# One slice's two layer-1 weight pieces converted by instructions over 1024 columns, and a query transposition that takes its result buffers itself

## The chip, the cores and the metric

The kernel runs on one core of a Trainium2 chip. A core has a matrix engine (TensorE, in the profile PE for matmuls and PEld for loading their weights), a vector engine (DVE), a scalar engine (ACT), GpSimd (POOL) and an engine that here only starts DMAs (SP). Each runs its own instructions in their order and waits on semaphores for the others. The metric is the device time of one execution in microseconds (us), lower is better. What is compared is the median of several runs; a profile is of one execution.

## The reference

```python
def _attn_ref(q, k, v, f):                      # 4 batches, 8 heads, 576 tokens, 64 per head
    scores = scale * np.matmul(q, k.transpose(0, 1, 3, 2))
    log_f = np.log(np.clip(f, 0.0001, 1.0))
    cum = np.cumsum(log_f, axis=-1)
    decay = cum[:, :, :, None] - cum[:, :, None, :]
    scores = np.where(causal, -1000000000.0, scores + decay)
    attn = softmax(scores)
    return np.matmul(attn, v)

def _moe_ref(x, w_in, w_out, alpha):            # layer 1: 2304 x 512, 512 x 2048, 2048 x 512
    h = x @ w_in
    g = np.maximum(h, 0.0) + alpha * np.minimum(h, 0.0)
    return g @ w_out

def _moe2_ref(x, w_in, w_out):                  # layer 2, same sizes
    h = x @ w_in
    g = np.where(h >= 1, h, np.where(h <= -1, 0.0, (h + 1) ** 2 / 4))
    return g @ w_out

def reference(...): return moe2(moe(attention(q, k, v, f)))
```

The weights arrive as 64-bit floats. The kernel has to make 32-bit values of them itself, from the two 32-bit words of each number.

## The kernel before

Attention runs batch by batch in units of 256 and 320 queries, and in each unit over four pairs of heads. The scores of a head (`ps_s`) are copied out by ACT with the decay as bias (L670), masked by POOL (L460), reduced to a maximum by DVE (L689, L707) and POOL (L713), subtracted (DVE, L729), exponentiated (ACT, L732) and multiplied with v (`ps_o`). The sums are inverted by way of a small DMA round trip (`rec`, `spread`, `sums`), and the result becomes a part of `x` (L837, L846, L849). The first batch uses plain 32-bit matmuls; from the second on operands are split in a high and a low part, as all of the weights and layer activations are.

Layer 1 goes through 9 chunks of 256 tokens and in each through 16 slices of 128 hidden units. For a slice, PE makes `ps_h` from the slice's part of w_in (12 matmuls, L979), ACT and DVE make `g` and its two parts (L989, L992, L998, L1001), and PE adds to `ps_y` with the slice's part of w_out (12 matmuls, L1018). Layer 2 takes the chunks in one narrow step of 256 tokens and four wide ones of 512 (`ps_h` L1154, `g` L1167 to L1182, `ps_z` L1201).

The weights of a layer come in 32 pieces of 128 x 512: piece 2s is the part of w_in for slice s, piece 2s + 1 that of w_out. A piece is loaded by SP (`raw`, L883), and then turned into 32-bit values: ACT writes the absolute value of the upper word to `val` (L894), DVE clamps it (L897), shifts it (L906), puts sign and top bits in (L914) and the lowest bits (L919), ACT copies the high part to `w` (L927) and DVE subtracts to get the low part (L932). Layer 1's pieces are done while attention begins, in buffers named `w0` to `w31` that hold raw words, `val` and at last `w` of different pieces one after the other; the raw words of piece i lie in the buffer of piece i + 2. Layer 2's pieces go to the same `w` buffers when the last chunk of layer 1 has used what is in them (`w_use`), by way of 3 raw and 14 `val` buffers.

The order of instructions on each engine is not that of the program text. Every step is a task with an engine, an assumed duration, a position (`pos`), dependencies and the ring buffers that it takes or uses. A planner (`Order.emit`) goes through assumed time, and gives each engine, whenever it is free, the task with the lowest position of those that can start. A task that takes a buffer is only given when one is free. Attention of the first batch has negative positions, conversions of layer 1 the position of their slice in the first chunk minus 9 or so, so that they fill what attention leaves. The waits in the program follow from the data and the buffers, not from the planner's assumed times.

Query transposition, from the second batch on: PE transposes the queries of a head into one of three PSUM buffers shared with the scores (`qtr`, L577), ACT copies the high part out (`qhi`) and DVE the low part (`qlo`); there are two result buffers per head of a pair, and it is `qhi` that takes them.

Of the kernel before, what the change touches and what calls it, by code (L numbers as in the profile page):

```python
# [16 lines left out]
P = 128  # L17
# [174 lines left out]
def kernel(  # L192
# [36 lines left out]
    AHEAD = 2  # L229
    THROTTLE = 8  # L230
    X2T = 768
# [232 lines left out]
    for u, pr in head_list():  # L464
# [104 lines left out]
        for j in range(0 if plain else 2):  # L569
# [18 lines left out]

            a = add("PE", 112 * np_, qtr, pos_of(2 * pr + j) - 1, [T["lq"], last.get("qtr")], new=[pb], use=[qb_])
            last["qtr"] = a  # L590
            h = add("ACT", act(n), qhi, pos_of(2 * pr + j) - 1, [a], new=qb, use=[pb])
            qready[j] = [h, add("DVE", dve(n), qlo, pos_of(2 * pr + j) - 1, [h], use=[pb, *qb])]
# [272 lines left out]
    W = {}  # L865
    W_ready = {}

    def convert(layer, i, pos, raw_ring, slot, deps, wdeps):
# [4 lines left out]
        there = layer == 1 and i + AHEAD < NPIECE  # L873
        vb = Buf(Ring(1) if there else R["val1" if layer == 1 else "val2"])
        keep = rb if there or not wide else vb

        def load():
            if part == 0:
                src = win[:, s * P:(s + 1) * P].rearrange("(c p) f -> p c f", p=P)
            else:  # L880
                src = wout[s * P:(s + 1) * P, :].rearrange("p (c f) -> p c f", f=P)
            rb.t = slot(rb)
            nc.sync.dma_start(out=rb.t, in_=src)  # L883
            if layer == 1 and i == 2:
                nc.sync.dma_start(out=alpha_sb, in_=alpha.rearrange("(s p) -> p s", p=P))

# [4 lines left out]
        def mag():  # L891
            pool, tag = (wpool, f"w{i}") if there else (ph["p"] if layer == 1 else P2["p"], f"val{vb.slot}")
            vb.t = pool.tile([P, DM], F32, tag=tag, name="val")
            nc.scalar.activation(out=vb.t, in_=words()[1].bitcast(F32), func=AF.Abs)  # L894
# [6 lines left out]
        def low_exp():  # L901
            if layer == 1 and i == 6:
                nc.vector.tensor_scalar(
                    out=calpha, in0=alpha_sb, scalar1=-1.0, scalar2=1.0, op0=ALU.mult, op1=ALU.add)
            bits = vb.t.bitcast(I32)
# [4 lines left out]
        def word():  # L910
            return words()[1] if there else vb.t.bitcast(I32)

# [12 lines left out]
        def hi():  # L925
            w = wpool.tile([P, 2, DM], F32R, tag=f"w{i}", name="w")
            nc.scalar.copy(out=w[:, 0, :], in_=val())  # L927
            W[layer, i] = (w[:, 0, :], w[:, 1, :])
# [7 lines left out]
        if wide:  # L936
            a = add("ACT", act(DM), mag, pos, [a] + (wdeps if layer == 1 else []), new=[vb], use=[rb])
            a = add("DVE", dve2(DM), clamp, pos, [a], use=[vb])
# [10 lines left out]
    raw_users = {}  # L949
    for i in range(NPIECE):  # L950
        def slot(b, i=i):
            return wpool.tile([P, NCC, P], WT, tag=f"w{i + AHEAD if i + AHEAD < NPIECE else i}", name="raw")

        r = convert(1, i, l1_pos[0, i // 2] + i % 2 / 2 - 1 + WOFF, Ring(1), slot,
                    raw_users.get(i - (THROTTLE if i + AHEAD < NPIECE else AHEAD), []),
                    raw_users.get(i - AHEAD, []))
        raw_users[i] = r
        conv1 += r
    for t in order.tasks:
        if "convert" in t.deps:  # L960
# [107 lines left out]
    for i in range(NPIECE):  # L1068
        conv2 += convert(2, i, NF * NC1 + i / 2 + WOFF2, R["raw2"],
                lambda b: P2["p"].tile([P, NCC, P], WT, tag=f"raw{b.slot}", name="raw"), [t_open], w_use[i])  # L1070

# [200 lines left out]
```

## Time and profile before

| | |
|---|---|
| runs (us) | 1062.47, 1063.72, 1067.35; median 1063.72 |
| profiled execution | 1062.05 us, its span 1060.3 us, mean granted clock of PE 0.985 |
| busy, share of the span | PE 96%, PEld 87%, DVE 71%, ACT 62%, POOL 14% |
| HBM | 61.42 MB read, 9.51 MB written |

The span goes from the first to the last instruction of the core; some 1.75 us of the execution lie outside of it. A busy share is an average over stages that have different limits: the first 160 us hold the first batch's attention and all of layer 1's conversion, up to some 560 us attention and layer 1 run side by side, and from 700 us on there is only layer 2.

### The profile page before, as it was taken

Reading aid. Unit: us, or ns where it says so; the run is one execution under the profiler, and the core shown is the slowest. Engines: PE = TensorE matmul, PEld = TensorE weight load, DVE = VectorE, ACT = ScalarE, POOL = GpSimd, SP = SyncE. Lnnn points to the kernel's source line nnn. Section 1 sums busy time; section 2 is a strip of 40 time slices with the busy share of each in tenths; the row PEclk is TensorE's granted clock in tenths of the full one; section 3 lists DMA queues with packets and bytes.
Section 4 is the critical chain, followed back from the end, with each engine's and each line's share of the span. In section 5 each row is a group of like instructions: output and inputs, shape, how many; then the busy total and the mean of one; then the engine's idle time right before and its main releaser. Section 6 shows DMA issues by size and latency. Waiting matters only on the chain.

```text
span 1060.3 us, 19265 instructions
## 1 busy us (share of the span) xinstructions
PE 1017.5 (96%) x6531; PEld 922.1 (87%) x6531; DVE 753.3 (71%) x1901; ACT 653.5 (62%) x1734; POOL 143.2 (14%) x239
## 2 busy tenths in 40 slices
PE   5679989999999999999999999999999999999998
PEld 3448879999999999999999999988888888888886
DVE  7989997787777787787757989974454445444443
ACT  6868778888888888987854465653343333333233
POOL 3323223211322113321200000000000000000000
PEclk9869999999999999999999999999999999999999
DMA  8774122311132111331105633521011001000001
GB/s 242 183 233 121 43 73 66 69 44 48 32 80 61 45 48 33 75 72 38 39 7 166 189 111 121 160 79 41 1 40 41 0 1 40 1 1 31 11 1 40
DMA packets 125650, 72.27 MB, mean 68 GB/s; under 512 B 89424, under 2 KB 119120, under 8 KB 125552
## 3 DMA queue, kind: packets, MB, share of 16 engines
q1 hardware_dynamic: 125552, 71.04, 24.6%
q8 instruction: 52, 0.85, 0.3%
q14 instruction: 46, 0.38, 0.1%
HBM read 61.42 MB, written 9.51 MB: 67 GB/s over the span
## 4 chain that ended last, share of the span: by engine, by line
PE 81%; DVE 5%; ACT 5%; issue 4%; DMA 3%; SPq 1%; POOL 1%; POOLq 0%; ACTq 0%; DVEq 0%
PE ps_h L1154 19%; PE ps_z L1201 18%; PE ps_y L1018 16%; PE ps_h L979 16%; PE ps_s L656 3%; PE ps_o L766 2%; PE ps_o L772 1%; PE ps_o L774 1%; PE ps_o L773 1%; PE pst L577 1%; DMA sums<-spread 1%; DMA spread<-rec 1%; SPq L404 1%; PE ps_s L652 1%; DMA raw<-in_k_dram 1%
## 5 line engine op out<-in xcount | busy, mean ns | idle before, releaser
L979 PE MATMUL ps_h<-x,w 128*128 128x256 f32 x1728 | 235.8, 286 | 4.3 <-DVE g L992 2.2
L1018 PE MATMUL ps_y<-gH,w 128*128 128x256 f32 x1152 | 236.3, 288 | 0.0
L979 PEld LDWEIGHTS ps_h<-x,w 128*128 128x128 f32 x1728 | 218.5, 192 | 6.5 <-DVE g L992 3.8
L1018 PEld LDWEIGHTS ps_y<-gH,w 128*128 128x128 f32 x1152 | 189.9, 192 | 0.2
L1154 PE MATMUL ps_h<-xw,w 128*128 128x512 f32 x768 | 184.5, 389 | 0.0
L1201 PE MATMUL ps_z<-w,gH 128*128 128x512 f32 x576 | 177.7, 389 | 0.0
L1154 PEld LDWEIGHTS ps_h<-xw,w 128*128 128x128 f32 x768 | 144.2, 188 | 29.9
L1018 PE MATMUL ps_y<-gL,w 128*128 128x256 f32 x576 | 163.7, 284 | 2.4 <-DVE gL L1001 2.4
L1179 ACT CAST gH<-g 128x256 fp32r<-128x256 f32 x144 | 58.5, 407 | 160.7 <-PE ps_z L1201 160.0
L1182 DVE TENSOR_TENSOR gL<-g,gH 128x256 fp32r<-128x256 f32 x144 | 61.0, 424 | 124.7 <-ACT gH L1179 124.5
L1201 PEld LDWEIGHTS ps_z<-w,gH 128*128 128x128 f32 x576 | 107.1, 188 | 21.4
L1171 ACT ACTIVATE g<-g,half 128x256 f32<-128x256 f32 x144 | 73.3, 509 | 69.9 <-DVE g L1167 69.6
L1018 PEld LDWEIGHTS ps_y<-gL,w 128*128 128x128 f32 x576 | 110.5, 192 | 3.3 <-DVE gL L1001 3.0
L1201 PE MATMUL ps_z<-w,gL 128*128 128x512 f32 x288 | 112.0, 389 | 0.0
L460 POOL TENSOR_SCALAR_AFFINE_SELECT S<-S 128x128 f32<-128x128 f32 (+1 forms) x160 | 61.3, 387 | 336.3 <-ACT S L670 319.7
L670 ACT ACTIVATE S<-ps_s,nb 128x320 f32<-128x320 f32 (+3 forms) x224 | 99.6, 449 | 11.3 <-PE ps_s L656 7.8
L992 DVE SCALAR_TENSOR_TENSOR g<-g,calpha,ps_h 128x256 f32<-128x256 f32 x144 | 68.3, 477 | 32.2 <-ACT g L989 31.4
L1174 DVE TENSOR_TENSOR g<-ps_h,g 128x256 f32<-128x256 f32 x144 | 61.0, 424 | 40.5 <-ACT g L1171 39.8
L713 POOL PARTITION_ALL_REDUCE Mb<-Mx x64 | 80.5, 1258 | 59.6 <-DVE Mx L707 24.2
L732 ACT ACTIVATE S<-S 128x320 f32<-128x320 f32 (+1 forms) x192 | 79.5, 423 | 11.7 <-DVE S L729 10.9
L729 DVE TENSOR_TENSOR S<-Mb,S 128x320 f32<-128x320 f32 (+3 forms) x224 | 78.7, 397 | 9.7 <-POOL Mb L713 9.1
L998 ACT CAST gH<-g 128x256 fp32r<-128x256 f32 x144 | 58.1, 405 | 42.4 <-DVE g L992 33.8
(100 smaller groups left out, 1607.8 us busy)
## 6 DMA issues: line engine op xcount, KB each, us to landing
raw<-in_moe_w_in_dram SPq DMA_DIRECT2D x32, 512.0 KB
raw<-in_moe_w_out_dram SPq DMA_DIRECT2D x32, 512.0 KB
x<-ysb SPq DMA_DIRECT2D x36, 128.0 KB
x<-x SPq DMA_DIRECT2D x9, 512.0 KB
out_dram<-osb SPq DMA_DIRECT2D x18, 256.0 KB
qr<-in_q_dram SPq DMA_DIRECT2D x64, 64.0 KB
raw<-in_k_dram SPq DMA_DIRECT2D x32, 128.0 KB
raw<-in_v_dram SPq DMA_DIRECT2D x24, 128.0 KB
```

Of the source, the lines that this page charges most:

```text
L460: nc.gpsimd.affine_select(out=sl, in_=sl, pattern=[[1, sl.shape[1]]], compare_op=ALU.is_ge, fill=NEG, base=base, channel_multiplier=-1)
L670: nc.scalar.activation(out=Sb.t[:, so:so + m], in_=sb.t[:, :m], func=AF.Identity, bias=bias)
L713: nc.gpsimd.partition_all_reduce(Mb.t[:, :n], Mx.t[:, :n], P, ReduceOp.max)
L729: nc.vector.tensor_tensor(out=sl, in0=Mb.t[:, qo:qo + m], in1=sl, op=ALU.subtract)
L732: ex = add("ACT", act(gn), lambda Sb=Sb, gn=gn: nc.scalar.activation(out=Sb.t[:, :gn], in_=Sb.t[:, :gn], func=AF.Exp, scale=-SCALE), pb_, ...
L979: nc.tensor.matmul(out=hb.t, lhsT=a[:, sl], rhs=b, start=(cc == 0 and t == 0), stop=(cc == NCC - 1 and t == 2))
L992: nc.vector.scalar_tensor_tensor(out=gb.t, in0=gb.t, scalar=calpha[:, s:s + 1], in1=hb.t, op0=ALU.mult, op1=ALU.add)
L1018: nc.tensor.matmul(out=Y[c][e // 2][:, e % 2, :], lhsT=a[:, sl], rhs=b, start=(s == 0 and t == 0 and e % 2 == 0), stop=(s == NF - 1 and t ...
L1154: nc.tensor.matmul(out=hb.t, lhsT=a[:, sl], rhs=b, start=(cc == 0 and t == 0), stop=(cc == NCC - 1 and t == 2))
L1171: nc.scalar.activation(out=gb.t, in_=gb.t, func=AF.Square, scale=0.5, bias=half)
L1174: nc.vector.tensor_tensor(out=gb.t, in0=hb.t[:, hs], in1=gb.t, op=ALU.max)
L1201: nc.tensor.matmul(out=zb[tg].t, lhsT=a[:, sl], rhs=b, start=(s == 0 and t == 0), stop=(s == NF - 1 and t == 2))
```

## The change

Slices 0 to 11 of layer 1 get one raw buffer for both pieces (still two DMAs), one `val` and one `w`, and each of the seven conversion steps is one instruction over 1024 columns. Slices 12 and 13 have their raw words in the four single buffers `p28` to `p31`, so that only the clamp and the shift are one instruction over 1024; their other five steps are two of 512 each. Slices 14 and 15 are converted piece by piece as before. Both pieces of a slice are ready together (`W_ready`), and the second load depends on the first in the planner. Layer 2's two pieces of slices 0 to 13 share one `w` buffer too, so each piece now waits for the last use of both. `qtr` now takes the two result buffers that `qhi` took. `THROTTLE` counts slices in place of pieces.

```diff
-    THROTTLE = 8
+    THROTTLE = 4
...
-            a = add("PE", 112 * np_, qtr, pos_of(2 * pr + j) - 1, [T["lq"], last.get("qtr")], new=[pb], use=[qb_])
+            a = add("PE", 112 * np_, qtr, pos_of(2 * pr + j) - 1, [T["lq"], last.get("qtr")], new=[pb] + qb, use=[qb_])
             last["qtr"] = a
-            h = add("ACT", act(n), qhi, pos_of(2 * pr + j) - 1, [a], new=qb, use=[pb])
+            h = add("ACT", act(n), qhi, pos_of(2 * pr + j) - 1, [a], use=[pb, *qb])
...
+    NWIDE = NF - 2 * AHEAD if wide else 0
+
+    def convert1(s, pos, deps, wdeps):
+        one = s < NWIDE
...
+                        rb.t = wpool.tile([P, 2, NCC, P], WT, tag=f"w{s + AHEAD}", name="raw")
...
+                nc.sync.dma_start(out=raws[-1][:, part if one else 0], in_=src)
...
+            loads.append(add("SP", 500, load, pos - 2 + part / 2, deps + loads, new=[] if part else [rb],
+                             use=[rb] if part else [], move=moved(P, 4096) if part else moved(NCC * P, 1024)))
...
+        n = 1 if one else 2
+        m = 2 * DM // n
+        a = add("ACT", n * act(m), lambda: each(mag), pos, loads + wdeps, new=[vb], use=[rb])
+        a = add("DVE", dve2(2 * DM), clamp, pos, [a], use=[vb])
+        a = add("DVE", dve2(2 * DM), low_exp, pos, [a], use=[vb])
+        a = add("DVE", n * dve(m), lambda: each(top), pos, [a], use=[vb, rb])
+        a = add("DVE", n * dve(m), lambda: each(bottom), pos, [a], use=[rb])
+        h = add("ACT", n * act(m), lambda: each(hi), pos, [a] + wdeps, use=[rb])
+        l = add("DVE", n * dve(m), lambda: each(lo), pos, [h], use=[rb])
+        W_ready[1, 2 * s] = W_ready[1, 2 * s + 1] = [h, l]
...
-            w = wpool.tile([P, 2, DM], F32R, tag=f"w{i}", name="w")
+            if s < NF - AHEAD:
+                if s not in WS2:
+                    WS2[s] = wpool.tile([P, 2, 2, DM], F32R, tag=f"w{s}", name="w")
+                w = WS2[s][:, part]
+            else:
+                w = wpool.tile([P, 2, DM], F32R, tag=f"p{i}", name="w")
...
+    for s in range(NF - AHEAD):
+        r = convert1(s, l1_pos[0, s] - 0.75 + WOFF, raw_users.get(s - THROTTLE, []), raw_users.get(s - AHEAD, []))
...
         conv2 += convert(2, i, NF * NC1 + i / 2 + WOFF2, R["raw2"],
-                lambda b: P2["p"].tile([P, NCC, P], WT, tag=f"raw{b.slot}", name="raw"), [t_open], w_use[i])
+                lambda b: P2["p"].tile([P, NCC, P], WT, tag=f"raw{b.slot}", name="raw"), [t_open],
+                w_use[i - i % 2] + w_use[i - i % 2 + 1])
```

Because the planner orders every engine anew, instructions move everywhere. The clamp is L914 in the new file, the shift L923, the next two L928 and L933, the low part L948 (L987, L993, L1001, L1006 and L1024 for single pieces); `g` of layer 1 is made by L1084 and L1093.

DVE at the start, from the prefix sum of f (L425) on; the numbers tell buffers apart (`val_207` is piece 0, `val_219` piece 1, `val_279` slice 0 of the new program). Before:

```order
L425 SCALAR_TENSOR_TENSOR cum_162<-raw0_123 32x576
L897 TENSOR_SCALAR val_207<-val_207 128x512
L906 TENSOR_SCALAR val_207<-val_207 128x512
L441 TENSOR_SCALAR nb_104<-pst_199 128x160
L914 SCALAR_TENSOR_TENSOR raw_172<-raw_172,val_207 128x512
L897 TENSOR_SCALAR val_219<-val_219 128x512
L919 SCALAR_TENSOR_TENSOR raw_172<-raw_172 128x512
L906 TENSOR_SCALAR val_219<-val_219 128x512
L689 TENSOR_TENSOR Mx_244<-S_223,S_228 128x128
L914 SCALAR_TENSOR_TENSOR raw_174<-raw_174,val_219 128x512
```

Now:

```order
L425 SCALAR_TENSOR_TENSOR cum_162<-raw0_123 32x576
L441 TENSOR_SCALAR nb_104<-pst_199 128x160
L689 TENSOR_TENSOR Mx_226<-S_209,S_214 128x128
L689 TENSOR_TENSOR Mx_245<-S_224,S_228 128x128
L729 TENSOR_TENSOR S_209<-Mb_240,S_209 128x256
L729 TENSOR_TENSOR S_214<-Mb_240,S_214 128x128
L729 TENSOR_TENSOR S_224<-Mb_255,S_224 128x256
L729 TENSOR_TENSOR S_228<-Mb_255,S_228 128x128
L914 TENSOR_SCALAR val_279<-val_279 128x1024
L923 TENSOR_SCALAR val_279<-val_279 128x1024
```

The decay bias nb, the maxima and the subtractions of both heads of the first pair now stand ahead of the first conversion, where two pieces were begun among them before.

SP at the start, the loads after those of the first head pair. Before:

```order
L883 DMA raw<-in_moe_w_in_dram 128x4x128
L883 DMA raw<-in_moe_w_out_dram 128x512
L883 DMA raw<-in_moe_w_in_dram 128x4x128
L885 DMA alpha_sb<-in_moe_alpha_dram 128x16x1
L404 DMA qr_110<-in_q_dram 128x2x64 x2
L404 DMA raw_124<-in_k_dram 128x2x64 x2
```

Now:

```order
L889 DMA raw<-in_moe_w_in_dram 128x4x128 x2
L891 DMA alpha_sb<-in_moe_alpha_dram 128x16x1
L889 DMA raw<-in_moe_w_in_dram 128x4x128
L404 DMA qr_110<-in_q_dram 128x2x64 x2
L404 DMA raw_124<-in_k_dram 128x2x64 x2
L889 DMA raw<-in_moe_w_in_dram 128x4x128
L889 DMA raw<-in_moe_w_out_dram 128x512 x3
```

The w_in parts of the first slices moved ahead, and the w_out parts behind the queries and keys of the second head pair.

DVE where layer 2's first weights are finished, in the last chunk of layer 1 (`ysb` is the output of the chunk before the last, `w` the low part of a weight piece). Before:

```order
L992 SCALAR_TENSOR_TENSOR g_9718<-g_9718,calpha_103,ps_h_9692 128x256
L1001 TENSOR_TENSOR gL_9722<-g_9718,gH_9721 128x256
L992 SCALAR_TENSOR_TENSOR g_9750<-g_9750,calpha_103,ps_h_9724 128x256
L932 TENSOR_TENSOR w_9752<-val_9169,w_9752 128x512
L1001 TENSOR_TENSOR gL_9757<-g_9750,gH_9756 128x256
L897 TENSOR_SCALAR val_9773<-val_9773 128x512
L906 TENSOR_SCALAR val_9773<-val_9773 128x512
L914 SCALAR_TENSOR_TENSOR val_9773<-raw_9607,val_9773 128x512
L992 SCALAR_TENSOR_TENSOR g_9789<-g_9789,calpha_103,ps_h_9759 128x256
L932 TENSOR_TENSOR w_9791<-val_9192,w_9791 128x512
L1035 COPY ysb_9814<-ps_y0_9171 128x256
```

Now:

```order
L1093 TENSOR_TENSOR gL_9658<-g_9654,gH_9657 128x256
L1127 COPY ysb_9676<-ps_y0_9039 128x256
L1127 COPY ysb_9680<-ps_y1_9040 128x256
L1084 SCALAR_TENSOR_TENSOR g_9713<-g_9713,calpha_103,ps_h_9660 128x256
L1084 SCALAR_TENSOR_TENSOR g_9728<-g_9728,calpha_103,ps_h_9683 128x256
L1024 TENSOR_TENSOR w_9730<-val_9080,w_9730 128x512
L1093 TENSOR_TENSOR gL_9734<-g_9713,gH_9733 128x256
L1093 TENSOR_TENSOR gL_9738<-g_9728,gH_9737 128x256
L1024 TENSOR_TENSOR w_9730<-val_9100,w_9730 128x512
L1024 TENSOR_TENSOR w_9756<-val_9122,w_9756 128x512
L1084 SCALAR_TENSOR_TENSOR g_9773<-g_9773,calpha_103,ps_h_9740 128x256
L1024 TENSOR_TENSOR w_9756<-val_9199,w_9756 128x512
```

The first low part moved from before the output copies of the chunk before the last to behind them, and then several follow at once.

## Rows read from the trace of the kernel before

**Rows 1.** Busy time by stretch: us, each engine (instructions), clock, DMA share, GB/s.

```profile
20.00:60.00 40.00, 26.73 (x88) 18.34 (x87) 38.67 (x88) 33.98 (x88) 15.52 (x21) 0.83 0.80 222
60.00:80.00 20.00, 14.14 (x47) 8.96 (x48) 16.81 (x41) 13.13 (x31) 3.98 (x6) 0.74 0.77 221
80.00:140.00 60.00, 58.11 (x388) 50.54 (x387) 59.22 (x145) 49.15 (x121) 18.59 (x23) 1.00 0.31 78
140.00:160.00 20.00, 16.37 (x112) 14.84 (x110) 19.46 (x47) 14.03 (x40) 4.99 (x11) 0.91 0.28 75
160.00:550.00 390.00, 386.61 (x3127) 382.78 (x3128) 301.51 (x827) 322.89 (x951) 93.68 (x162) 1.00 0.22 52
550.00:1060.00 510.00, 504.06 (x2743) 439.32 (x2741) 304.02 (x724) 208.34 (x483) 0.00 (x0) 1.00 0.18 56
```

**Rows 2.** Groups by line, 0 to 160 us: count, busy us, mean ns, idle before.

```profile
L914 DVE SCALAR_TENSOR_TENSOR raw<-raw,val 128x512 int32<-128x512 int32 x30 | 22.8, 760 | 0.3
L897 DVE TENSOR_SCALAR val<-val 128x512 f32<-128x512 f32 x32 | 15.0, 468 | 2.8 <-ACT val L894 2.7
...
L894 ACT ACTIVATE val<-raw 128x512 f32<-128x512 f32 x32 | 21.5, 675 | 8.5 <-DVE w L932 5.0 <-DMA raw<-in_moe_w_in_dram 1.9 <-DMA vF<-in_v_dram 0.8
```

**Rows 3.** DVE in order of time: start, length (us), instruction.

```profile
688.42 0.69 DVE L914 SCALAR_TENSOR_TENSOR val<-raw,val 128x512 int32<-128x512 int32 x1
689.02 0.69 DVE L932 TENSOR_TENSOR w<-val,w 128x512 fp32r<-128x512 f32 x1
689.62 0.42 DVE L1174 TENSOR_TENSOR g<-ps_h,g 128x256 f32<-128x256 f32 x1
689.96 0.42 DVE L1167 TENSOR_SCALAR g<-ps_h 128x256 f32<-128x256 f32 x1
...
691.56 0.42 DVE L897 TENSOR_SCALAR val<-val 128x512 f32<-128x512 f32 x1
691.89 0.69 DVE L932 TENSOR_TENSOR w<-val,w 128x512 fp32r<-128x512 f32 x1
```

**Rows 4.** ACT in order of time at the start.

```profile
15.42 0.67 ACT L894 ACTIVATE val<-raw 128x512 f32<-128x512 f32 x1
15.99 0.65 ACT L927 CAST w<-raw 128x512 fp32r<-128x512 f32 x1
16.66 1.28 ACT L732 ACT_TABLE_LOAD   x1
17.95 0.42 ACT L732 ACTIVATE S<-S 128x256 f32<-128x256 f32 x1
18.27 0.28 ACT L697 COPY Mx<-S 128x128 f32<-128x128 f32 x1
```

**Rows 5.** The first 20 us by stretch, and DVE in order of time there.

```profile
0.00:10.00 10.00, 4.49 (x15) 2.68 (x15) 5.38 (x18) 3.59 (x7) 2.00 (x10) 1.00 0.63 189
10.00:20.00 10.00, 6.93 (x19) 4.62 (x20) 8.19 (x18) 8.36 (x20) 4.42 (x7) 1.00 0.91 236
...
9.28 0.43 DVE L897 TENSOR_SCALAR val<-val 128x512 f32<-128x512 f32 x1 [2.14 <-ACT val L894]
...
10.09 0.32 DVE L441 TENSOR_SCALAR nb<-pst 128x160 f32<-128x160 f32 x1
```

**Rows 6.** DVE and PE in order of time, from layer 1 to layer 2.

```profile
616.05 0.69 DVE L932 TENSOR_TENSOR w<-val,w 128x512 fp32r<-128x512 f32 x1
...
624.99 0.68 DVE L932 TENSOR_TENSOR w<-val,w 128x512 fp32r<-128x512 f32 x1
...
625.11 1.60 PE L979 MATMUL ps_h<-x,w 128*128 128x256 f32 x12
...
695.93 0.69 DVE L932 TENSOR_TENSOR w<-val,w 128x512 fp32r<-128x512 f32 x1 [0.35 <-ACT w L927]
...
697.91 1.59 PE L1154 MATMUL ps_h<-x,w 128*128 128x256 f32 x12
...
704.81 2.88 PE L1154 MATMUL ps_h<-xw,w 128*128 128x512 f32 x12
```

More of the change, by code (lines that the diff above doesn't have):

```diff
@@ L871, in convert @@
         rb = Buf(raw_ring)
-        there = layer == 1 and i + AHEAD < NPIECE
-        vb = Buf(Ring(1) if there else R["val1" if layer == 1 else "val2"])
-        keep = rb if there or not wide else vb
+        vb = Buf(R["val1" if layer == 1 else "val2"])
+        keep = vb if wide else rb
         def load():
@@ L883, in load @@
             nc.sync.dma_start(out=rb.t, in_=src)
-            if layer == 1 and i == 2:
-                nc.sync.dma_start(out=alpha_sb, in_=alpha.rearrange("(s p) -> p s", p=P))
         def words():
@@ L891, in mag @@
         def mag():
-            pool, tag = (wpool, f"w{i}") if there else (ph["p"] if layer == 1 else P2["p"], f"val{vb.slot}")
-            vb.t = pool.tile([P, DM], F32, tag=tag, name="val")
+            vb.t = (ph["p"] if layer == 1 else P2["p"]).tile([P, DM], F32, tag=f"val{vb.slot}", name="val")
             nc.scalar.activation(out=vb.t, in_=words()[1].bitcast(F32), func=AF.Abs)
@@ L901, in low_exp @@
         def low_exp():
-            if layer == 1 and i == 6:
-                nc.vector.tensor_scalar(
-                    out=calpha, in0=alpha_sb, scalar1=-1.0, scalar2=1.0, op0=ALU.mult, op1=ALU.add)
             bits = vb.t.bitcast(I32)
@@ L910, in word @@
         def word():
-            return words()[1] if there else vb.t.bitcast(I32)
+            return vb.t.bitcast(I32)
         def top():
@@ L925, in hi @@
         def hi():
[L926 removed]
+            if s < NF - AHEAD:
+                if s not in WS2:
+                    WS2[s] = wpool.tile([P, 2, 2, DM], F32R, tag=f"w{s}", name="w")
+                w = WS2[s][:, part]
+            else:
+                w = wpool.tile([P, 2, DM], F32R, tag=f"p{i}", name="w")
             nc.scalar.copy(out=w[:, 0, :], in_=val())
@@ L936, in convert @@
         if wide:
-            a = add("ACT", act(DM), mag, pos, [a] + (wdeps if layer == 1 else []), new=[vb], use=[rb])
+            a = add("ACT", act(DM), mag, pos, [a], new=[vb], use=[rb])
             a = add("DVE", dve2(DM), clamp, pos, [a], use=[vb])
@@ L949 @@
     raw_users = {}
[L950 to L957, printed above, removed]
+    assert wide
+    for s in range(NF - AHEAD):
+        r = convert1(s, l1_pos[0, s] - 0.75 + WOFF, raw_users.get(s - THROTTLE, []), raw_users.get(s - AHEAD, []))
+        raw_users[s] = r
         conv1 += r
+    for i in range(2 * (NF - AHEAD), NPIECE):
+        before = raw_users[i // 2 - AHEAD]
+        conv1 += convert(1, i, l1_pos[0, i // 2] + i % 2 / 2 - 1 + WOFF, Ring(1),
+                         lambda b, i=i: wpool.tile([P, NCC, P], WT, tag=f"p{i}", name="raw"), before, before)
     for t in order.tasks:
```

60 lines of the change are left out of this document (added).

## The prediction

> **What bounds the kernel now.** I read the busy times by stretch first, then the groups of the conversion, then single instructions in order of time on DVE and ACT, and last the order of the changed program. In the stretches [rows 1] the reader is to see that TensorE (PE) sets the end from 160 us on: it is busy 386.6 of 390 us up to 550 and 504.1 of the last 510. What PE loses, it loses early: 13.3 of 40 us between 20 and 60, 5.9 of 20 between 60 and 80, 1.9 of 60 between 80 and 140, 3.6 of 20 between 140 and 160. In the same stretches DVE is busy 38.7 of 40, 16.8 of 20, 59.2 of 60 and 19.5 of 20 us. So up to 160 us DVE is the engine that everything waits for, first behind the attention of the first batch, then behind the weights of layer 1, and PE idles or is granted its lower level part of the time (0.74 of the clock between 60 and 80). The change takes work from just this engine in just this stage. The work PE must do stays the same, so each microsecond by which the DVE-bound stage gets shorter is a microsecond off the end, as long as PE has other idle time there to give up.
>
> **The wide conversion, on DVE.** Before, a piece of 128x512 takes five DVE instructions (clamp L897, shift L906, L914, L919, L932) and two on ACT (L894, L927); 32 pieces make 160 and 64 [rows 2]. After, twelve slices take 5 + 2 each, two slices share only the clamp and the shift (8 + 4 each), and four pieces stay as they were (20 + 8): 60 + 16 + 20 = 96 on DVE and 24 + 8 + 8 = 40 on ACT. So 64 DVE and 24 ACT instructions go, while the columns stay the same. What one costs beyond its columns is read from starts, since the next instruction starts before the one in front has ended: a two-source instruction over 512 columns holds DVE 0.60 us (688.42 to 689.02), one over 256 columns 0.34 us (689.62 to 689.96), and a clamp over 512, which runs at twice the rate, 0.33 us (691.56 to 691.89) [rows 3]. 256 columns more cost 0.26 us, so the part without columns is 0.60 - 2 x 0.26, about 0.07 us. 64 x 0.07 is 4.5 us of DVE. On ACT 512 columns hold it 0.57 us (15.42 to 15.99) and 256 columns 0.32 us (17.95 to 18.27) [rows 4], which leaves 0.07 us, times 24 is 1.7 us; ACT is not full in that stage (34.0 of 40 us, then 49.2 of 60 [rows 1]), so I count these at nothing.
>
> The trace has no instruction over 1024 columns. By the line above one holds DVE 1.13 us, a clamp 0.60. The bounds for the saving: nothing, if the wide form costs what two narrow ones do, and 64 x 0.17 = 11 us, if not the distance but the whole length of an instruction held DVE (0.69 us long against 0.60 apart [rows 3], and 0.69 - 2 x 0.26 = 0.17). I take 4.5, since the starts show the difference overlapped. [...]
>
> **What the wide form delays.** A slice can only start when both of its pieces have landed, and the kernel's planner, which knows that, puts the second load behind the first. In the new SP order the first three w_out loads stand behind the q and k loads of the second head pair; before, the first piece pair stood ahead of them. And in the new DVE order no conversion stands before the four subtractions of the first pair, whereas before the clamp of piece 0 started at 9.28 [rows 5]. On ACT the first val copy now stands behind the four exponentials of the first pair; in the trace the first of these starts at 17.95, right after the table load [rows 4], so I expect the first conversion on DVE near 18 to 19 us. Up to 20 us the kernel before had done 13 conversion instructions on DVE (six single-source at 0.33, seven two-source at 0.60, 6.2 us) of the 13.6 us that DVE was busy [rows 5]. These 6.2 us move to a time when DVE is full. Against it stands that nb (L441), which the scores wait for, ran at 10.09 behind a clamp that had idled DVE 2.1 us for its load [rows 5]; without it the first pair's chain can begin some 2 us sooner, and DVE's idle 3.2 us between 60 and 80 [rows 1] can take in part of what was put off. So this term lies between 6.2 us lost and 2 us won; I take 2 us lost, since most of the weights are not due until the first 256 tokens are through attention, and the order up to that point carries two to three pieces fewer and no less attention.
>
> **The query transposition.** It now waits on PE's side for its two result buffers; before, it filled one of the three score buffers in PSUM and sat in it until ACT could copy it. This matters from the second batch on, where PE loses 3.4 us in 390 [rows 1]: at most that can be won, and the same size lost where a transposition now comes too late for its head; matmuls of layer 1 stand behind it on PE and in front of it, so I count it at nothing.
>
> **The second layer's weights.** Their buffers are now the slice's, shared by both pieces, so a piece of w_in waits for the last use of w_out as well. In the last chunk of layer 1 the first split result (L932) was written at 616.05, after the h matmuls of slice 0; now it waits for that slice's y matmuls, which end where the row at 625.11 starts [rows 6]. The 14 val buffers are full by then, so DVE's conversions stop for these 9 us. What stood in them: five L932, two L897, two L906, one L914, one L919 (from 616.05 to 624.99 [rows 6]), 6 x 0.60 + 4 x 0.33 + 0.60 = 5.5 us, put off into a stretch in which DVE is full until 696. The last h weights were ready at 692.6 (L932 at 691.89 [rows 3]) and used at 697.91, the last of all at 696.6 (695.93), with the wide chunks beginning at 704.81 [rows 6]. 5.5 us late is 698.1 and 702.1: 0.2 us after the first of these uses. The new PE order puts four more z groups ahead of the last narrow h, and all 32 ahead of the first wide one (27 before); four are 2.7 us of cover. So between 0 and 5.5 us, and I take 0.5.
>
> **Sum.** -4.5 + 2.0 + 0 + 0.5 = -2.0 us on the profiled execution: 1062.05 to 1060.05 (span 1060.3 to 1058.3, the 1.75 around it unchanged). That execution is the fastest seen; the median of the three shown is 1063.72, 1.7 above. I start from the middle of the two, 1063.0 rounded, for a typical run: 1061.0 us.
>
> **Rivals.** *The start gets much shorter.* PE idles or is slowed most before 80 us. If attention, no longer interleaved with conversions from the first microseconds, brings the first 256 tokens through earlier, PE gets back a third of the 19 us that it loses between 20 and 80, in place of the 2 us lost above: -4.5 - 6 = -10.5, with the 0.5 still against it -10, 1053.0. For it: the new PE order has nine more attention rows ahead of the first h. Against it: the last links of that chain are DMAs, which fewer DVE instructions do not shorten.
> *A whole length is saved per instruction,* not a distance: -11 + 2 + 0.5 = -8.5, 1054.5. Against it: the starts in [rows 3]. [...]
> *The time freed is not on the path:* DVE's 4.5 us go into the idle time created before 19 us and the end stays at 1063.0. For it: PE is itself busy 58.1 of 60 us between 80 and 140 [rows 1].
> *Slower: conversions that start late stay late.* The 6.2 us come back in full at 140 to 160, where PE already runs out of weights, and the second layer's weights miss their use by 5 us: -4.5 + 6.2 + 5 = +6.7, 1069.7. It decides once the gap before the first conversion exceeds 4.5 us, or L932 of the last h piece ends after PE has reached its h.
>
> **How the numbers follow.** What a measurement of this kernel can tell from no change is 0.5%, 5.3 us: below 1058.4 is faster, above 1069.0 slower. Chances: the forecast, -1 to -5 us, 0.42; the short start 0.24; the whole length 0.05; nothing moves 0.13; slower 0.16. Faster takes the second and third and a little of the first, 0.31; slower most of the last plus a little for orders I have not followed, 0.16; the rest, 0.53, is no change. The range goes from 1051 (the short start and a little more) to 1069.5 (the slower case up to its middle). The forecast's own is 1057 to 1065.
>
> **What would show it.** Right: instructions over 1024 columns 1.13 us apart and clamps 0.60; the last layer-1 L948 or L1024 no later than 160 us with three more layer-1 slices done by then; PE's loss between 140 and 160 below 3.6 us; the first layer-2 split near 625 and no wait of PE for weights near 700. Wrong: wide instructions more than 1.2 us apart; a first clamp later than 20 us; PE idle between 20 and 80 above 19 us; PE waiting at the last narrow h.

## The result, and the profile after

The changed kernel takes 1069.78 us (median of 6 runs, 1069.30 to 1071.07), the kernel before 1063.53 (6 runs): a ratio of 1.0055, 95% interval 1.0039 to 1.0071. It is slower, where I forecast 1061.0, and 0.3 us outside the range. The profiled execution took 1069.94 us with a span of 1068.2, against 1062.05 and 1060.3.

By stretches, as in [rows 1] and [rows 5] (length, then busy us and instructions of each engine, clock, DMA share, GB/s):

```profile
10.00:20.00 10.00, 5.02 (x15) 3.21 (x15) 2.81 (x7) 6.24 (x15) 3.21 (x5) 1.00 0.95 303
20.00:60.00 40.00, 26.83 (x91) 18.15 (x89) 38.09 (x66) 34.28 (x82) 18.49 (x21) 0.76 0.67 186
60.00:80.00 20.00, 15.26 (x41) 10.40 (x42) 18.99 (x34) 14.06 (x25) 6.29 (x8) 0.64 0.62 176
80.00:140.00 60.00, 57.09 (x387) 50.41 (x386) 59.18 (x123) 48.94 (x118) 17.41 (x20) 1.00 0.39 112
140.00:160.00 20.00, 17.17 (x133) 15.79 (x132) 18.99 (x46) 14.04 (x39) 6.00 (x10) 1.00 0.29 82
160.00:550.00 390.00, 384.64 (x3106) 378.85 (x3105) 303.65 (x825) 322.21 (x945) 93.66 (x164) 1.00 0.23 51
```

The first clamp came as forecast, but not the short start that was a rival: layer 1's first h starts at 79.72, where it started at 73.31. Between 140 and 160 us PE does 133 matmuls where it did 112, at the full clock, and up to 220 us it has done 1168 against 1137. At some 0.12 us each (59.40 us for 490 between 160 and 220) those 31 are at most 3.8 us of lead (what is ahead is layer 1, what is behind is attention, whose matmuls over 320 columns took 0.30 to 0.33 us where layer 1's over 256 took 0.28 to 0.29, before, between 160 and 220). Then it goes: PE idles 5.4 us between 160 and 550, where it idled 3.4. By 660 us the lead is gone, and PE stands where it stood; what is lost in the end is lost in the next 80 us. Up to 660 and from there to 740, before and then after:

```profile
0.00:660.00 660.00, 621.33 (x4686) 590.45 (x4687) 541.90 (x1383) 502.67 (x1386) 143.16 (x239) 0.98 0.34 89
660.00:740.00 80.00, 79.59 (x452) 69.78 (x451) 60.59 (x149) 40.25 (x93) 0.00 (x0) 1.00 0.32 99
```

```profile
0.00:660.00 660.00, 621.30 (x4688) 589.75 (x4689) 534.53 (x1307) 498.77 (x1357) 147.62 (x239) 0.97 0.33 88
660.00:740.00 80.00, 75.02 (x420) 64.91 (x419) 62.79 (x154) 40.61 (x94) 0.00 (x0) 0.98 0.37 112
```

The 32 matmuls that are missing there are of layer 2, most of them over 512 columns at 0.23 us each (12 start within 2.72 us): some 7 of the 7.9 us by which the span is longer.

The conversion groups that answer to [rows 2], of the stretch from 0 to 160 us (count | busy us, mean ns):

```profile
L933 DVE SCALAR_TENSOR_TENSOR raw<-raw 128x1024 int32<-128x1024 int32 x12 | 15.1, 1257 | 0.0
L948 DVE TENSOR_TENSOR w<-raw,w 128x1024 fp32r<-128x1024 f32 x12 | 15.1, 1256 | 0.0
L914 DVE TENSOR_SCALAR val<-val 128x1024 f32<-128x1024 f32 x14 | 11.2, 804 | 5.5 <-ACT val L911 5.5
```

And DVE in order of time, at the start and where layer 1 is under way (start, length, what, idle time before it):

```profile
13.63 0.62 DVE L729 TENSOR_TENSOR S<-Mb,S 128x256 f32<-128x256 f32 x2 [0.34 <-POOL Mb L713]
19.73 0.69 DVE L914 TENSOR_SCALAR val<-val 128x1024 f32<-128x1024 f32 x1 [5.47 <-ACT val L911]
...
104.19 0.68 DVE L923 TENSOR_SCALAR val<-val 128x1024 int32<-128x1024 int32 x1
104.79 0.68 DVE L914 TENSOR_SCALAR val<-val 128x1024 f32<-128x1024 f32 x1
105.39 0.41 DVE L1093 TENSOR_TENSOR gL<-g,gH 128x256 fp32r<-128x256 f32 x1
105.73 1.22 DVE L928 SCALAR_TENSOR_TENSOR raw<-raw,val 128x1024 int32<-128x1024 int32 x1
106.86 0.16 DVE L820 TENSOR_SCALAR rec<-rec 128x5 f32<-128x5 f32 x1
```

A wide two-source instruction holds DVE 1.13 us (105.73 to 106.86), a wide clamp or shift 0.60 (104.19 to 104.79 to 105.39): the distances read off [rows 3]. Against the 0.60 and 0.33 us over 512 columns there, 512 columns more cost 0.53 and 0.27. The first clamp comes at 19.73.

What the prediction had not looked at is the change from attention to layer 2. SP's issues there, before:

```profile
561.87 0.54 SPq L1110 DMA_DIRECT2D x<-x  x1
562.46 0.50 SPq L883 DMA_DIRECT2D raw<-in_moe_w_in_dram  x1
...
569.81 3.13 SPq L1039 DMA_DIRECT2D x<-ysb  x4
```

and after:

```profile
570.13 1.80 SPq L1131 DMA_DIRECT2D x<-ysb  x4
572.01 0.41 SPq L1203 DMA_DIRECT2D x<-x  x1
572.47 0.55 SPq L976 DMA_DIRECT2D raw<-in_moe_w_in_dram  x1
```

The last values of attention (L846) were started at 565.58 and are now started at 570.00: the lead went into layer 1 (200 ps_h matmuls between 160 and 220 us against 168), not into attention (38 ps_s of L656 against 48). As layer 1's seventh chunk now ends ahead of the attention, its four output stores stand in front of layer 2's first weight loads, which go out 10 us later. The first val copy of layer 2 starts at 578.75, before at 571.17.

The rows that answer to [rows 6], DVE and then PE (a split is the last conversion step of a layer-2 piece, the low part, L1024 now and L932 before):

```profile
625.05 0.69 DVE L1024 TENSOR_TENSOR w<-val,w 128x512 fp32r<-128x512 f32 x1
...
703.56 0.69 DVE L1024 TENSOR_TENSOR w<-val,w 128x512 fp32r<-128x512 f32 x1
...
708.75 0.39 PE L1294 MATMUL ps_z<-w,gL 128*128 128x512 f32 x1
710.35 6.08 PE L1247 MATMUL ps_h<-xw,w 128*128 128x512 f32 x24 [1.22 <-ACT xw L1217]
718.70 4.57 PE L1247 MATMUL ps_h<-xw,w 128*128 128x512 f32 x12 [2.28 <-DVE g L1267]
```

The first split comes at 625.05, 9 us later, as forecast; the last at 703.56, 7.6 later; the first wide h at 710.35, 5.5 later. There PE waits for the wide step's input (1.22 us) and for g (2.28), as all z matmuls of the narrow step are already behind it, and then runs its next 12 matmuls in 4.57 us where 12 took 2.88: after these waits the granted clock was 0.50 from 720 to 723 us (0.92 on average between 720 and 740, before 1.00). By the program, the wide step's input lies in memory that the conversion's buffers give back. ACT makes the first of its eight parts 1.0 us after the last split has ended (704.25), and stands still for z before the other seven:

```profile
705.26 0.40 ACT L1217 CAST xw<-x 128x256 fp32r<-128x256 f32 x1
708.49 0.59 ACT L1309 COPY osb<-ps_z 128x512 f32<-128x512 f32 x1 [2.83 <-PE ps_z L1294]
708.98 2.24 ACT L1217 CAST xw<-x 128x256 fp32r<-128x256 f32 x7
```

The copy of the narrow step's output (`osb`) is in front of them in the new order; before, all eight were made from 700.77 on, ahead of the first such copy. (An order with these copies alone put back was not tried, so what share the late split and the copy have each is not shown.) From the first wide h to the end of the span are 355.5 us before (704.81 to 1060.3) and 357.9 now. What this kernel's wide step waits for is therefore a chain beside PE: end of attention, loads, conversion on DVE, input of the wide step, first wide h.

### The profile page after: what moved, and what is told of

It is laid out like the page before. It is cut to its first block, busy times and chain, and to the rows that moved or that the text cites. A ratio compares the mean times of both kernels' runs of the same rounds, so it can differ in the third digit from the quotient of the medians.

```text
span 1068.2 us, 19128 instructions
## 1 busy us (share of the span) xinstructions
PE 1019.6 (95%) x6531; PEld 922.1 (86%) x6531; DVE 750.1 (70%) x1837; ACT 652.7 (61%) x1710; POOL 147.6 (14%) x239
## 4 chain that ended last, share of the span: by engine, by line
PE 74%; DVE 12%; ACT 6%; issue 4%; DMA 2%; POOL 1%; SPq 0%; POOLq 0%; ACTq 0%; DVEq 0%
PE ps_z L1294 18%; PE ps_h L1247 18%; PE ps_y L1110 15%; PE ps_h L1071 14%; PE ps_s L656 3%; DVE S L729 2%; PE ps_o L766 2%; PE ps_o L772 1%; DVE kT L542 1%; PE ps_o L774 1%; PE ps_o L773 1%; POOL Mb L713 1%; DVE w L948 1%; ACT S L732 1%; PE pst L577 1%
## 5 line engine op out<-in xcount | busy, mean ns | idle before, releaser
L713 POOL PARTITION_ALL_REDUCE Mb<-Mx x64 | 84.2, 1315 | 79.6 <-DVE Mx L707 32.7
L1084 DVE SCALAR_TENSOR_TENSOR g<-g,calpha,ps_h 128x256 f32<-128x256 f32 x144 | 68.4, 476 | 30.2 <-ACT g L1081 29.5
```

Of the source, the lines that this page charges most:

```text
L713: nc.gpsimd.partition_all_reduce(Mb.t[:, :n], Mx.t[:, :n], P, ReduceOp.max)
L1084: nc.vector.scalar_tensor_tensor(out=gb.t, in0=gb.t, scalar=calpha[:, s:s + 1], in1=hb.t, op0=ALU.mult, op1=ALU.add)
```

## The experiments

Each ratio is to the kernel before, run beside it on the same chip, with its 95% interval; where times of different groups are compared, it is by these ratios.

**Layer 2's wait, alone and taken out.** Three kernels. The first is the kernel before with this edit alone; its `w` buffers stay single, so only the order made from the assumed wait changes, and the orders of PE, DVE and ACT differ only from 615 us on:

```diff
-                lambda b: ..., [t_open], w_use[i])
+                lambda b: ..., [t_open], w_use[i - i % 2] + w_use[i - i % 2 + 1])
```

> The kernel before, with only the planner's wait of layer 2's pieces set to both uses of the slice (the buffers stay single, the order of the attention and of layer 1's conversion stays). First split at about 625 in place of 616, last at about 704 in place of 696.6. Theory W: 5 to 6 us slower than the kernel before, 1068 to 1069. Rival (postponed work is taken up in DVE's free time, the 0.5 us of my prediction): within 1 us of the kernel before.

1068.33 against 1063.20, ratio 1.0050 (1.0036 to 1.0064). This one line by itself makes a loss of 5.1 us, and at the wide step its trace is that of the changed kernel:

```profile
623.79 0.69 DVE L932 TENSOR_TENSOR w<-val,w 128x512 fp32r<-128x512 f32 x1
...
703.95 0.69 DVE L932 TENSOR_TENSOR w<-val,w 128x512 fp32r<-128x512 f32 x1 [0.34 <-ACT w L927]
...
710.51 6.08 PE L1154 MATMUL ps_h<-xw,w 128*128 128x512 f32 x24 [1.22 <-ACT xw L1124]
719.11 4.53 PE L1154 MATMUL ps_h<-xw,w 128*128 128x512 f32 x12 [2.52 <-DVE g L1174]
```

The other two take it out of the changed kernel: layer 2 writes into the halves of the buffer that is there, and the planner is told so (first; called own waits below, as against the change's shared wait), or not (second):

```diff
-                    WS2[s] = wpool.tile([P, 2, 2, DM], F32R, tag=f"w{s}", name="w")
-                w = WS2[s][:, part]
+                w = WS[s][:, part]
...
-                w_use[i - i % 2] + w_use[i - i % 2 + 1])      # first kernel only
+                w_use[i])
```

> The changed kernel, but layer 2 writes each piece into the layer-1 buffer that is there already, and a piece waits for the last use of its own half alone, for the planner and on the chip. Up to 600 us all orders are those of the changed kernel. Theory A (the shared wait of the second layer's weights makes the kernel slower): the first layer-2 split comes at about 616 again in place of 625.1, the last at or before 697 in place of 703.6, PE no longer waits 1.2 and 2.3 us behind the narrow chunk, and the time is 6 us below the changed kernel's, about 1063.8. Theory B (query transposition or the late start of the conversion is what costs): the time stays within 1.5 us of 1069.8.

> The changed kernel with the buffer wait of layer 2 alone taken out: each piece goes into its half of the buffer that is there, but the planner still believes that it waits for both uses, so PE's order is the changed kernel's to the last row. Theory A1 (the wait itself costs): the first split runs before 625 and the time falls by 4 to 6 us, to about 1065. Theory A2 (the order that the planner makes because of the wait costs: all z matmuls of the narrow step ahead of the first wide h, and the output copies ahead of the wide step's input): the time stays within 1.5 us of 1069.8 and PE still waits about 1.2 and 2.3 us at the first wide h.

1066.89 (ratio 1.0039, 1.0024 to 1.0054) and 1069.25 (1.0062, 1.0046 to 1.0077). The buffer freed without a new order brings nothing: the first split still comes at 625.4. So what costs is the order, not the buffer. (The order for own waits on a shared buffer was not tried.) But the new order brings only about 1.7 us here, where 6 were expected (and the intervals of 1.0055 and 1.0039 overlap): with the conversion starting at 579.34, the last split comes at 698.38, 2.5 us later than before, and PE idles 4.0 us between 600 and 680 (1.9 us for layer 1's g, 2.1 for layer 2's first), as DVE, busy 78.8 of these 80 us where it was 75.5 before, makes g late. Something else was late: the start of the conversion.

**Start of layer 2's loads, by hand.** Three kernels that change SP's order alone: the four stores of layer 1's seventh chunk held back until the third weight load is issued (changed kernel, with shared and with own waits), or these three loads held back until the stores are issued (kernel before).

```diff
-                nc.sync.dma_start(out=to, in_=yb.t)
+                if c == 6:
+                    held.append((to, yb.t))    # issued behind layer 2's third load
+                else:
+                    nc.sync.dma_start(out=to, in_=yb.t)
```

> The changed kernel; SP issues the four stores of layer 1's seventh chunk behind the first three weight loads of layer 2 and not ahead of them (the order that the kernel before had), all other orders as they were. The loads then go out at about 567 in place of 572.5, and the first val copy comes at about 573 in place of 578.8. Theory S (the end of layer 2's conversion follows its start): the last split comes 5 us earlier than 704.3 and the time falls by 4 to 5 us, to about 1065. Theory W (the shared wait holds the splits until 625, and the 14 val buffers are full by then either way): last split at 704 as before, time within 1.5 us of 1069.8.

> The changed kernel with both: the three loads ahead of the stores, and each layer-2 piece waiting for the last use of its own half alone. If start and wait each stand in the other's way, this is better than both single steps together: first split near 616, last at 694 to 697, no wait of PE behind the narrow chunk; 4 us below the kernel with its own wait alone (1066.9), about 1062.5, which is level with the kernel before. If a third thing is behind the loss, it stays above 1065.

> The kernel before, with only the first three weight loads of layer 2 moved behind the four stores of layer 1's seventh chunk in SP's order (all else as it was). The loads go out at about 573 in place of 562.5, the first val copy at about 578 in place of 571.2. Theory S: the last split moves from 696.6 to 699 or later, PE waits some 3 us more in layer 2's narrow step, 1066 to 1067. If the start has slack (the 14 val buffers are full before the first split anyway): within 1 us of the kernel before, 1062.5 to 1063.5.

1072.36 (1.0085), 1069.11 (1.0055), 1070.08 (1.0064): all three slower, and none tells the theories apart, because the rest of the order did not fit. In the first the loads go out at 565.97, 6.5 us earlier, and yet the first val copy comes at 578.76, where 573 was expected; in the second it comes at 581.18. In these two layer 1's g waits 3.87 and 5.15 us on ACT for the buffers of the stores, which are issued behind 1.5 MB of weights, and the val copies come after it. In the third, ACT shows what a late load does (rows of ACT):

```profile
569.72 1.33 ACT L1131 CAST x<-x 128x256 fp32r<-128x256 f32 x4
576.47 0.66 ACT L898 ACTIVATE val<-raw 128x512 f32<-128x512 f32 x1 [5.41 <-DMA raw<-in_moe_w_in_dram]
...
580.21 0.64 ACT L993 ACTIVATE g<-ps_h 128x256 f32<-128x256 f32 x2
```

The val copy waits 5.4 us for its load, the g of layer 1 stands behind it, and PE stops for 7.8 us. So moving the loads alone does not move the conversion; the next group lets the planner do it.

**Attention sooner.** `RATE` is the distance of a batch's attention positions; 30 in place of 31 lets attention end sooner against layer 1, and the loads come ahead of the stores again without any hand. With own waits, with the shared wait, and in the kernel before:

```diff
-    RATE = 31
+    RATE = 30
```

> The changed kernel with layer 2's own waits (as the first experiment) and the attention of the later batches given positions a little closer together (RATE 30 in place of 31), so that it ends sooner against layer 1 and SP's order has the first three layer-2 loads ahead of the four stores of layer 1's seventh chunk, as the kernel before had. Nothing is held back by hand. If the start of layer 2's conversion (579.3 with own waits against 571.2 before) is what is left of the loss once the shared wait is gone: first val copy at 569 to 574, last split at 691 to 696, no wait of PE in the narrow step, and 4 to 6 us below 1066.9, so 1061 to 1063. If a third thing costs it: 1065 or more.

> The changed kernel with RATE 30 alone; the shared wait stays. Up to layer 2's splits its order is that of the run with own waits and RATE 30. Theory W (the shared wait holds the splits until the y matmuls of slice 0, however early the conversion starts): first split 620 to 625, last 702 to 704, time 1068 to 1070. If the start alone were enough: 1064 or less.

> The kernel before with RATE 30 alone: attention ends earlier against layer 1, layer 1's matmuls come later. If the end of the attention, and not PE's total work, sets layer 2's conversion and so the end: first val copy 3 to 7 us earlier than 571.2, and 2 to 5 us faster, 1058 to 1061. If the own wait for slice 0 in the last chunk (first split 616) sets it, or PE's work does: 1063 within 1.5.

With own waits 1064.55 (1.0014, 1.0003 to 1.0025), with the shared wait 1070.28 (1.0061, 1.0046 to 1.0077), the kernel before 1061.96 (0.9984, 0.9974 to 0.9994). With the two of the first group this is a table of four: late start of layer 2's conversion and shared wait 1.0055, late start and own wait 1.0039, early start and shared wait 1.0061, early start and own wait 1.0014. Neither single step gives much, both together bring 4.4 of 5.8 us: with the shared wait the first split comes at 627.29 though the conversion starts 6.0 us earlier (572.74), and with the late start PE waits for g, as above. (The intervals of the two with the late start overlap, those of the two with own waits touch; the last stands clear of both with the shared wait.) The rows with both:

```profile
575.57 1.81 ACT L984 ACTIVATE val<-raw 128x512 f32<-128x512 f32 x3
...
620.30 0.69 DVE L1024 TENSOR_TENSOR w<-val,w 128x512 fp32r<-128x512 f32 x1
...
700.19 0.69 DVE L1024 TENSOR_TENSOR w<-val,w 128x512 fp32r<-128x512 f32 x1 [0.35 <-ACT w L1019]
...
709.06 2.88 PE L1247 MATMUL ps_h<-xw,w 128*128 128x512 f32 x12
```

PE no longer waits at the wide step, and between 600 and 680 it idles 0.4 us in place of 4.0. The last split fell no earlier than 700.19 (expected were 691 to 696, and 1061 to 1063 for the time), so it is not the time of the last split alone that counts, but whether PE runs out of work. What is left of the loss lies ahead of layer 2: between 500 and 550 PE does 371 matmuls, in the kernel before 404, and attention's last values come 3.5 us later (569.04). In the kernel before, RATE 30 brought the first val copy 2.3 us sooner (568.89), and the time fell by 1.7 us by the ratio, less than the 2 expected; its last split came no earlier (696.70), so from where the gain comes its profile does not show.

**The width alone.** The changed kernel, and later the best one, with each conversion step of slices 0 to 13 as two instructions over 512 columns; loads, buffers and order stay:

```diff
         def clamp():
-            nc.vector.tensor_scalar(out=vb.t, in0=vb.t, ...)
+            for x in range(2):
+                nc.vector.tensor_scalar(out=vals(x), in0=vals(x), ...)
```

> The changed kernel, same loads, buffers and order of steps, but every conversion step of slices 0 to 13 is two instructions of 512 columns. The theory of the prediction (64 DVE instructions at 0.07 us are 4.5 us of an engine that is full until 160 us, all of it on the path): 1074, with layer 1's last split 4.5 us later. Rival (DVE's saved time is not on the path, or the width saves nothing): within 1.5 us of 1069.8.

> The fastest kernel so far (own waits, RATE 29, LEAD 7), its order unchanged, but two instructions of 512 columns in each conversion step of slices 0 to 13. If the 4.9 us of the wide instructions reach the end here: 1065 to 1066. If the end is set by something that the start does not move: 1061 to 1062.

1073.59 (1.0101, 1.0083 to 1.0118) where the changed kernel has 1.0055, and 1066.66 (1.0028, 1.0017 to 1.0038) where the best has 0.9973. So the width is worth 0.46% or 4.9 us, and 0.55% or 5.8 us (give or take some 2.5 and 1.7 us by the intervals; the second is the firmer). PE's order is the same to the last row in each pair, and the loss travels whole: layer 2's first val copy comes at 584.51 against 578.75, and at 573.99 against 568.08. The changed kernel, and then the one with halves, from 0 on:

```profile
0.00:160.00 160.00, 126.87 (x678) 101.71 (x679) 143.20 (x288) 121.13 (x283) 53.95 (x76) 0.89 0.53 149
160.00:220.00 60.00, 59.40 (x490) 58.51 (x489) 46.60 (x128) 48.49 (x149) 14.26 (x28) 1.00 0.26 61
```

```profile
0.00:160.00 160.00, 120.73 (x651) 96.98 (x651) 140.49 (x339) 118.62 (x293) 53.75 (x72) 0.90 0.53 148
160.00:220.00 60.00, 57.67 (x466) 56.04 (x467) 46.60 (x129) 48.18 (x149) 15.38 (x31) 1.00 0.25 57
```

Up to 220 us 51 matmuls fewer with halves, and 20 fewer than the kernel before (1137): the slice-wise order by itself costs some 2.4 us there, at 0.12 each.

**The query transposition.** Undone in the changed kernel, and done alone in the kernel before:

```diff
-            a = add("PE", ..., qtr, ..., new=[pb] + qb, use=[qb_])
+            a = add("PE", ..., qtr, ..., new=[pb], use=[qb_])
...
-            h = add("ACT", act(n), qhi, ..., [a], use=[pb, *qb])
+            h = add("ACT", act(n), qhi, ..., [a], new=qb, use=[pb])
```

> The changed kernel with the query transposition as it was before. If the transposition's buffers cost what the changed kernel gives back between 250 and 550 us (by its matmul counts about 3 to 4 us), the time is 3 to 4 us lower, about 1066. If it is worth nothing, as I predicted, the time is 1069.8 within 1.5 us.

> The kernel before with the query transposition's change alone. The changed kernel without it was 2.9 us slower than with it (ratios 1.0082 and 1.0055). If that gain is a property of the edit, this is 3 us faster than before, 1060. If it came from how the planner happens to order attention and layer 1 (its SP order here has the layer-2 loads behind the stores, as in the changed kernel), layer 2's conversion starts late, at 576 or later, and the time is 2 to 5 us above before, 1065 to 1068.

1071.98 (1.0082, 1.0065 to 1.0099): undone, the changed kernel is about 2.9 us slower, though the intervals overlap. 1076.28 (1.0117, 1.0102 to 1.0132): alone, it makes the kernel before 12.4 us slower by the ratio, more than the 2 to 5 expected: between 300 and 320 us PE is busy 15.8 of 20 us at 0.83 of the clock (19.0 at 1.00 before), and the first val copy of layer 2 moves from 571.2 to 586.3. So the edit has no price of its own that these two runs agree on; what it costs or gains depends on the order around it.

**The late first conversion.** The run with own waits and RATE 30, its loads unchained, and the same with layer 1's conversions one position earlier:

```diff
-            loads.append(add("SP", 500, load, pos - 2 + part / 2, deps + loads, ...
+            loads.append(add("SP", 500, load, pos - 2 + part / 2, deps, ...
...
-    WOFF = -8
+    WOFF = -9      # second kernel only
```

> The run with own waits and RATE 30, and in addition the planner no longer puts a slice's second load behind its first: the first conversion stands ahead of the first pair's maxima again, so the first clamp comes at about 10 to 12 us in place of 19.7. By term 2 of the prediction (2 us lost, bounds 6.2 lost and 2 won) PE is 2 us further on at 200 us than in the run with RATE 30 alone. If the conversions held back are taken in by DVE's free time before 80 us, PE stands where it did within 1 us. The whole time: 1062 to 1064 by the first, 1064 to 1065.5 by the second.

> As the run with unchained loads, and layer 1's conversions one position earlier (WOFF -9). Same two outcomes: 1060 to 1062 if the early start and the wide instructions reach the end, 1064 or more if not.

1070.24 (1.0057) and 1066.57 (1.0030), both slower than 1.0014: wrong in sign. The first clamp comes at 11.32 as it should, but by 220 us PE has done 1091 matmuls, against 1156 with the late clamp. SP's last return of the first 256 tokens' sums (L828), unchained and then with the late clamp:

```profile
75.50 1.12 SPq L828 DMA_DIRECT2D sums<-spread  x2
```

```profile
69.43 1.13 SPq L828 DMA_DIRECT2D sums<-spread  x2
```

The return comes 6 us later, and so does layer 1's first h (89.17 against 81.30). At the start one sees why: two wide two-source instructions (13.24 and 15.08) get in between, and the first pair's subtractions start at 16.22 in place of 12.38. Letting attention go first was a gain in this order, though the planner's order changed in other places as well.

**The best version.** Own waits, and two numbers found among settings for which the planner ends attention early; then the same numbers in the kernel before, and the best with the shared wait:

```diff
-    LEAD = 8
-    RATE = 31
+    LEAD = 7
+    RATE = 29
```

> The changed kernel with own waits, RATE 29 and LEAD 7 (attention of the later batches starts a position later and ends sooner). If the 3 us gained by 200 us can be carried to the end: attention's last values by 565, first val copy by 571, last split by 694, and 1060 to 1062, below the kernel before (1063.2). If what is won at the start is spent on layer 1 whatever the positions are: 1064 to 1066.

> The kernel before with RATE 29 and LEAD 7 alone. If the positions bring the gain by themselves: 1060 to 1062. If they only let the wide conversion's gain through: 1063 or more.

> The changed kernel with RATE 29 and LEAD 7, layer 2's shared wait as the change has it. If the wait costs in every order what it cost alone on the kernel before: first split 9 us later than the best kernel's 614.6, last split 8 us later than 695.6, 5 us slower, about 1066. If the earlier end of the attention makes up for it: 1062 or less.

The first takes 1060.87 (0.9973, 0.9960 to 0.9985): faster than both kernels, by 0.3% and 0.8%. Its rows along the chain:

```profile
556.73 0.50 SPq L976 DMA_DIRECT2D raw<-in_moe_w_in_dram  x1
...
568.08 0.66 ACT L984 ACTIVATE val<-raw 128x512 f32<-128x512 f32 x1
...
614.56 0.69 DVE L1024 TENSOR_TENSOR w<-val,w 128x512 fp32r<-128x512 f32 x1
...
694.89 0.69 DVE L1024 TENSOR_TENSOR w<-val,w 128x512 fp32r<-128x512 f32 x1 [0.35 <-ACT w L1019]
...
703.77 2.88 PE L1247 MATMUL ps_h<-xw,w 128*128 128x512 f32 x12
```

Every link stands 1 to 6 us ahead of the kernel before, and from the first wide h to the end are 355.4 us, as there. The numbers alone make the kernel before slower, 1080.83 (1.0156): its attention then ends 22.7 us later. With the shared wait the best kernel takes 1063.13 (0.9994, 0.9984 to 1.0005), so the wait costs 0.21% or 2.2 us here, less than the 5 expected; with RATE 30 it was 0.47%, on the kernel before 0.50%.

## Why the prediction was wrong

*Wide conversion, -4.5.* Right. The distances were 1.13 and 0.60 us as worked out, and the width is worth 4.9 and 5.8 us in two kernels, 0.08 and 0.09 per instruction saved. The upper bound of 11 us, with the whole length of an instruction (0.69 us over 512 columns) holding DVE, is not borne out: what counts here is the distance of starts (0.60).

*Late start, +2.* Near in size to the cost of the slice-wise order (some 2.4 us by the matmuls done with halves), but by luck, as the cause was wrong: starting the conversion sooner cost more still in the two orders tried. The sign that I had named, the last split of layer 1 by 160 us, failed (164.2) without harm.

*Query transposition, 0.* A gain of 2.9 us in this order and a loss of 12 in another; my bounds of 3.4 came from PE's idle time alone and left out that a new order can move the end of attention.

*Layer 2's wait, +0.5.* This is the step that failed. I put the postponed work at 5.5 us (the last split came 7.6 us later, and 8.0 with this edit alone), took the uses of the h weights as the only thing that is late next, and took "all 32 z groups ahead of the first wide h" for cover. It is the opposite: with these z matmuls used up, PE has nothing left to do while the wide step's input and its first g are made. That input comes after the last split and behind an output copy that waits for z, a path that the prediction did not look at. The edit alone, on the kernel before, cost 5.1 us where I took 0.5.

*"Each microsecond by which the DVE-bound stage gets shorter is a microsecond off the end."* Within one order this holds: the two kernels with halves lose at the end about what they lose at the start. Across the change it failed, because every engine got a new order, and this is the more general step. The lead that was there at 220 us was gone by 660: the order spent it on layer 1, attention ended 4.4 us later, and layer 2's loads went out 10 us later. I read "PE is busy" from 160 us on as "PE sets the end" in any order, and did not look at the hand-over in the new one, where the chain from attention's end over DVE to the first wide h makes PE wait.

*The slower rival* gave 6.7 us where 6.3 were measured, which is luck in part, as one of its two reasons was wrong: nothing came back between 140 and 160 us, where PE's loss fell from 3.6 to 2.8 us. The miss in layer 2 was real, at another place: the wide step's input, not the last h piece.

What is not settled: how much of the loss belongs to which edit. The costs do not add (the shared wait costs 1.7 to 5.1 us by kernel, the query edit -2.9 to +12.4), as each edit gives a new order; why, edit by edit, stays open.

## What to carry to other kernels

Where a planner or list scheduler orders the work, a gain in an early stage is only a gain if it reaches the next hand-over: look up what each later stage waits for first (here the end of attention and the last split), and follow that in the new order, SP's queue included, before counting anything. A wait that is told to the planner can cost by the order that comes of it, even where the buffer never waits; and filler work that an engine has finished early is no cover for a later wait. Test a saved cost by undoing it within the new order (two halves in place of one), since the edit alone in the old order measures the order.

## What the runs showed of the hardware

Of the 28 clamps and shifts over 1024 columns in the changed kernel, the six that started while an all-reduce of GpSimd ran, 0.3 us or more before its end, took 0.89 to 1.21 us; the other 22 took 0.68 to 0.82. DVE and then POOL:

```profile
99.43 1.20 DVE L914 TENSOR_SCALAR val<-val 128x1024 f32<-128x1024 f32 x1
...
130.50 0.68 DVE L923 TENSOR_SCALAR val<-val 128x1024 int32<-128x1024 int32 x1
```

```profile
99.20 1.88 POOL L713 PARTITION_ALL_REDUCE Mb<-Mx  x1 [1.31 <-DVE Mx L707]
...
130.67 1.61 POOL L713 PARTITION_ALL_REDUCE Mb<-Mx  x1 [1.98 <-DVE Mx L707]
```

The first started 0.23 us into an all-reduce and took 1.20 us, nearly twice the 0.68 of the second; it was not held until the all-reduce ended (100.63 against 101.08). Three others that started inside one took about as long (1.10 us at 31.99, 1.20 at 89.56, 1.21 at 110.17), and two that started 0.34 and 0.41 us before its end took 0.89 and 0.96 (33.12, 90.80). The second started 0.17 us before an all-reduce and took 0.68 us. Three of the long ones are clamps and most of why the mean of L914 is 804 ns (1.5 of the 1.7 us that the 14 take above 0.68 each). (GpSimd's spans in a profile are rough.)
